# Clustered attention and MLP on one core: a fourth staging buffer, two copies on GpSimd, and the exponential's bias on ScalarE

## The chip, the cores and the metric

The kernel runs on one core of a Trainium2 chip. The core has a matrix engine (TensorE; PE in the profile, with its weight loads under PEld), three engines for elementwise work (VectorE or DVE, ScalarE or ACT, GpSimd or POOL), a queue for DMAs (SyncE or SP) and 16 DMA engines. Each engine takes its instructions in order and waits on semaphores for the others. The metric is device time in microseconds of one execution. The time before is 1006.37 us, the median of 3 runs from 1002.96 to 1007.54.

## The reference

Attention in which a query sees only keys of its own cluster, followed by an MLP with a squared relu:

```python
B, H, S, D = 4, 8, 768, 64            # 16 clusters a head
q_assign = argmax(einsum('bhsd,hcd->bhsc', q_n, c_n))      # rows normalized
k_assign = argmax(einsum('bhsd,hcd->bhsc', k_n, c_n))
scores = (q @ k.T) / sqrt(D); scores = where(q_assign == k_assign, scores, -1e9)
attn = exp(scores - max(scores)); attn = attn / (sum(attn) + 1e-9)
x = (attn @ v) rearranged to (B*S, H*D) = (3072, 512)
h = x @ w_in                           # (512, 2048)
out = (s * relu(h)**2 + b) @ w_out     # (2048, 512)
```

All inputs and the output are float32. `w_in` and `w_out` arrive as 8-byte elements (the kernel reads them as pairs of 32-bit integers), 16 MB in all.

## The kernel before

**Split numbers.** To keep float32 accuracy at the matrix engine's float16 speed, every operand is held as a high half and a low half in float16, and a product takes three matmuls (high with high, high with low, low with high). For the scores, a key tile `ka` holds high and low halves side by side (128 columns), a second one `kb` holds the high halves again beside a column block with the key's one-hot cluster; the queries have `qa` (low halves, and a copy of the high halves) and `qb` (high halves, and the one-hot). A DMA transpose turns each of the four into `KA`, `KB`, `QA`, `QB`. So `QA` times `KA` plus `QB` times `KB` is the whole masked score.

**Units and steps.** The attention is cut into 192 units of 128 queries by 768 keys. In turn `i` of the main loop (line 699) unit `i` gets its scores (`scores`, L455), its maxima (`maxima`, L464), and its exponential (`exps`, L471 and L474); unit `i-1` gets the high half of its probabilities (`high`, L119) and the low half (`low`, L497) and goes through a DMA transpose to `PT` (L499); two units at a time are multiplied by the values (`values`, L516 to L518) and normalized (L524 to L528). The MLP runs 21 turns behind (`LAG`): step `m = i - 21` takes one of 16 blocks of the hidden layer for 256 tokens: `mlp_in` (L574), relu and two squares on ScalarE (L581 to L584), the low half on GpSimd (L589), and `mlp_out` (L601). The last 21 steps of the MLP have no attention beside them.

**Weights.** `weights()` is a loop over 32 tiles, `w_in` and `w_out` in turn, that is advanced two turns with each turn of the main loop (three at the start). `fetch` takes a 512 KB tile into a staging buffer `wst` (tag "stage", 3 buffers); `rebase` (L203, L205, ScalarE) and `narrow` (L209, L210, VectorE) make float32 out of the 8-byte elements; `bound` collects the magnitudes (L216 or L221, L222) and puts the sign back (L223, GpSimd). Tile `i` is fetched in turn `i`, rebased and narrowed in turn `i+2`, bounded in turn `i+3`. The split of the weights into halves (`wsplit`, L267 and L269) needs the bounds over all tiles, and is called from turn 17 on, one block a turn.

**Keys and queries.** `prep_k` and `prep_q` load, find the scale, split (`split`, L185 on ScalarE and L187 on VectorE), copy the high halves to their second place (L325 for keys, L375 for queries, both VectorE), start the transposes of `ka` and `qa` (L329, L379), compute the cluster assignments (`onehot`, L288 to L294) and start the transposes of `kb` and `qb` (L342, L392). For the first batch they run partly ahead of the main loop; for the others they are spread over the turns of the batch before. `kb` of batch 0's first pair of heads and of all pairs of batches 1 to 3 is one tile that is kept for the whole kernel (`kb_kept`), so that a copy into it must wait until the transpose out of it (L342) has landed. Other large working tiles (`p`, `ph`, `PT`, `qn`, `qa`, `qb`, `ka`) share 11 buffers of tag "big".

**Order.** A planner orders the instructions of each engine from the order of the program, priorities (the first 20 units come first) and its own estimate of times, and sets the semaphores. DMAs are all issued on SP, in order, so one that waits for its buffer holds up those behind it. `last_split` holds the last instructions of the latest split, behind which some early preparation is ordered.

Of the kernel before, what the change touches and what calls it, by code (L numbers as in the profile page):

```python
# [8 lines left out]
F16 = mybir.dt.float16  # L9
BF16 = mybir.dt.bfloat16  # L10
F32 = mybir.dt.float32
I32 = mybir.dt.int32
U32 = mybir.dt.uint32
AF = mybir.ActivationFunctionType
ALU = mybir.AluOpType
# [11 lines left out]
def tile_cluster_attention_mlp(ctx, tc, q, k, v, cent, w_in, w_out, s_in, b_in, out):  # L27
# [28 lines left out]
    def const(shape, dt, name):  # L56
        return cp.tile(shape, dt, tag=name, name=name)
# [120 lines left out]
    def split(hi, lo, src, f, early):  # L178
        if early:
            A.activation(src, src, AF.Copy, scale=f)  # L180
            last_split[1] = A.activation(hi, src, AF.Copy)
            yield
            G.tensor_tensor(lo, src, hi, op=ALU.subtract)
        else:
            last_split[1] = A.activation(hi, src, AF.Copy, scale=f)  # L185
            yield
            V.scalar_tensor_tensor(lo, src, f, hi, op0=ALU.mult, op1=ALU.subtract)  # L187

    def fetch(p):
        ft = p // 2  # L190
        if p % 2 == 0:
            w = wi[ft] = weight_tile(f"wi{ft}")
            src = w_in.bitcast(I32)[:, ft * 2 * P : (ft + 1) * 2 * P].rearrange("(t p) f -> p t f", p=P)
        else:
            w = wo[ft] = weight_tile(f"wo{ft}")
            src = w_out.bitcast(I32)[ft * P : (ft + 1) * P, :].rearrange("p (a f) -> p a f", a=KT)
        st = sb.tile([P, KT, P, 2], I32, tag="stage", name=f"wst_{p}", bufs=3)
        load(st.rearrange("p a f w -> p a (f w)"), src)
        return {"w": w, "st": st, "p": p, "ft": ft}

# [27 lines left out]

    def weights():
        live = {}  # L230
        for i in range(2 * NF + 3):
            if 0 <= i - 3:
                bound(live[i - 3])
                narrowed[0] += 1
            if 0 <= i - 2 < 2 * NF:
                rebase(live[i - 2])
                narrow(live[i - 2])
            if i < 2 * NF:
                live[i] = fetch(i)
            if i < 2 * NF + 2:  # L240
                yield

    def finish_w_in():
# [52 lines left out]
    KS = {}  # L296
    KSM = {}
    QS = {}
    kb_kept = const([P, 2, T, 2, D], F16, "kb")

    def prep_k(b, hp):
        kb = kb_kept
        if b == 0 and hp > 0:
            kb = sb.tile([P, 2 * T, P], F16, tag="big", name=f"kb_{hp}", bufs=BIGN).rearrange("p (h t) (e d) -> p h t e d", h=2, e=2)
        n = f"{b}_{hp}"
        kn = sb.tile([P, 2, T, D], F32, tag="kv", name=f"kn_{n}", bufs=5)
        load(kn, k[b, 2 * hp : 2 * hp + 2].rearrange("h (p t) d -> p h t d", t=T))
        yield
        if hp == 0:
            KSM[b] = sb.tile([P, 4, NP], F32, tag="ksm", name=f"ksm_{n}", bufs=2)  # L310
        sm = [KSM[b][:, e, hp : hp + 1] for e in range(4)]
        km = columns(1, f"k{n}")
        absmax(km, kn.rearrange("p h t d -> p (h t d)"))
        if b:
            yield
        allmax(sm[1], km, f"k{n}", "m" if b or not hp else "h")
        yield
        scale2(sm[2], sm[1])
        inverse2(V, sm[3], sm[2], 22)
        if b == 0 and hp > 0:  # L320
            ka = sb.tile([P, 2 * T, P], F16, tag="big", name=f"ka_{hp}", bufs=BIGN).rearrange("p (h t) (e d) -> p h t e d", h=2, e=2)
        else:
            ka = sb.tile([P, 2, T, 2, D], F16, tag="big", name=f"ka_{n}", bufs=BIGN)
        yield from split(ka[:, :, :, 0, :], ka[:, :, :, 1, :], kn, sm[2], False)
        last_split[0] = V.tensor_copy(kb[:, :, :, 0, :], ka[:, :, :, 0, :])  # L325
        KA = sb.tile([P, 2 * T, P], F16, tag="KA", name=f"KA_{n}", bufs=5)
        KB = sb.tile([P, 2 * T, P], F16, tag="KB", name=f"KB_{n}", bufs=5)
        KS[(b, hp)] = (KA, KB)
        last_turn[0] = nc.sync.dma_start_transpose(KA, ka.rearrange("p h t e d -> p (h t e d)"))  # L329
        yield  # L330
        yield
        pa = (ps_m if b or not hp else ps_h).tile([P, 512], F32, tag="m" if b or not hp else "h", name=f"pk_{n}")
        for h in range(2):
            hc = slice((2 * hp + h) * C, (2 * hp + h + 1) * C)
            for t in range(T):
                i = h * T + t
                o = pa[:, i * C : (i + 1) * C]
                nc.tensor.matmul(o, KA[:, i, :], cT[:, 0, hc], start=True, stop=False)
                nc.tensor.matmul(o, KA[:, i, :], cT[:, 1, hc], start=False, stop=True)
        mk = kb.rearrange("p h t e (r c) -> p (h t) e r c", c=C)[:, :, 1, :, :]  # L340
        yield from onehot(pa, 2 * T, f"k{n}", mk, BIG, -BIG)
        last_turn[0] = nc.sync.dma_start_transpose(KB, kb.rearrange("p h t e d -> p (h t e d)"))  # L342

    def prep_q(b, c, hq):
        n = f"{b}_{c}_{hq}"
        nh = 4
        qn = sb.tile([P, 2 * T * P // 2], F32, tag="big", name=f"qn_{n}", bufs=BIGN)[:, : nh * CT * D].rearrange("p (h t d) -> p h t d", h=nh, t=CT)
        load(
            qn, q[b, nh * hq : nh * hq + nh].rearrange("h (p t) d -> p h t d", t=T)[:, :, c * CT : (c + 1) * CT, :]
        )  # L350
        yield
        prs = slice(2 * hq, 2 * hq + 2)
        sm = sb.tile([P, 4, 2], F32, tag="qsm", name=f"qsm_{n}", bufs=3)
        qm = columns(2, f"q{n}")
        absmax(qm, qn.rearrange("p (j h) t d -> p j (h t d)", j=2))
        if b + c:
            yield
        allmax(sm[:, 1, :], qm, f"q{n}", "m" if b or c else "h")
        yield
        f = sm[:, 2, :]  # L360
        scale2(f, sm[:, 1, :])
        V.tensor_tensor(f, f, KSM[b][:, 3, prs], op=ALU.min)
        V.tensor_tensor(sm[:, 1, :], f, KSM[b][:, 2, prs], op=ALU.mult)
        inverse2(V, sm[:, 3, :], sm[:, 1, :], -3)
        qa = sb.tile([P, 2 * T * P], F16, tag="big", name=f"qa_{n}", bufs=BIGN)[:, : nh * CT * 2 * D].rearrange("p (h t e d) -> p h t e d", h=nh, t=CT, e=2)
        qb = sb.tile([P, 2 * T * P], F16, tag="big", name=f"qb_{n}", bufs=BIGN)[:, : nh * CT * 2 * D].rearrange("p (h t e d) -> p h t e d", h=nh, t=CT, e=2)
        both = []
        for j in range(2):
            hs = slice(2 * j, 2 * j + 2)
            both.append(split(qb[:, hs, :, 0, :], qa[:, hs, :, 0, :], qn[:, hs], sm[:, 2, j : j + 1], b + c == 0))  # L370
        for z in zip(*both):
            yield
        for z in both:
            next(z, None)
        V.tensor_copy(qa[:, :, :, 1, :], qb[:, :, :, 0, :])  # L375
        QA = sb.tile([P, nh * CT, P], F16, tag="QA", name=f"QA_{n}", bufs=2)
        QB = sb.tile([P, nh * CT, P], F16, tag="QB", name=f"QB_{n}", bufs=2)
        QS[(b, c, hq)] = (QA, QB, sm)
        nc.sync.dma_start_transpose(QA, qa.rearrange("p h t e d -> p (h t e d)"))  # L379
        yield  # L380
        yield
        pa = (ps_m if b or c else ps_h).tile([P, 512], F32, tag="m" if b or c else "h", name=f"pq_{n}")
        for h in range(nh):
            hc = slice((nh * hq + h) * C, (nh * hq + h + 1) * C)
            for t in range(CT):
                i = h * CT + t
                o = pa[:, i * C : (i + 1) * C]
                nc.tensor.matmul(o, QA[:, i, :], cT[:, 0, hc], start=True, stop=False)
                nc.tensor.matmul(o, QA[:, i, :], cT[:, 2, hc], start=False, stop=True)
        mk = qb.rearrange("p h t e (r c) -> p (h t) e r c", c=C)[:, :, 1, :, :]  # L390
        yield from onehot(pa, nh * CT, f"q{n}", mk, BIG, 0.0)
        nc.sync.dma_start_transpose(QB, qb.rearrange("p h t e d -> p (h t e d)"))  # L392
# [41 lines left out]
                    yield  # L434


    LIFT = 14.0 * math.log(2.0)
    units = [(b, c, hp, t, h) for b in range(B) for c in range(NCH) for hp in range(NP) for t in range(CT) for h in range(2)]
    NU = len(units)
    U = {}  # L440
# [25 lines left out]
    def exps(i):  # L466
# [1 line left out]
        sm = SM[i // 4]  # L468
        bi = sm[:, 1, j : j + 1]
        u = U[i]  # L470
        V.tensor_scalar(bi, sm[:, 0, j : j + 1], u["scale"], LIFT, op0=ALU.mult, op1=ALU.add)  # L471
        p = sb.tile([P, S], F32, tag="big", name=f"p_{i}", bufs=BIGN)
        total = {"accum_out": sm[:, 2, j : j + 1]} if i < RAW else {}
        last_exp[0] = A.activation(p.rearrange("p (a b) -> p a b", a=2), u["sc"], AF.Exp, bias=bi, scale=u["scale"], **total)  # L474
# [117 lines left out]
    def mlp_out(b, c, ft):  # L592
# [9 lines left out]
                                 start=(ft == 0 and gl + wl == 0), stop=(ft == NF - 1 and gl == 1))  # L602
        if ft == NF - 1:
            _, e, acc = MS.pop((b, c))
            o = sb.tile([P, CT, DM], F32, tag="stage", name=f"o_{n}", bufs=3)
            if b + c == 0:
                column_sums()
            for t in range(CT):
# [151 lines left out]
```

## Time and profile before

| | us | |
|---|---|---|
| median of 3 runs | 1006.37 | 1002.96 to 1007.54 |
| the profiled execution | 1002.93 | its span is 1001.3 |
| mean granted TensorE clock | 0.932 | of full speed |

The profile is of one execution. Its page gives busy times of the engines, the span in 40 slices, the chain of work that ended last, and groups of instructions. A group's row names the line, the engine, the operation, the tiles out and in with their shapes and the count, then the total busy us and the mean ns of one, then the idle time of its engine just before them with what ended it:

```profile
L464 DVE TENSOR_REDUCE ssm<-sc 128x1 f32<-128x768 f32 x192 | 181.3, 949 | 24.9 <-PE sc L455 24.8
L474 ACT ACTIVATE p<-sc,ssm,qsm 128x768 f32<-128x768 f32 x192 | 188.4, 981 | 63.0 <-DVE ssm L471 37.2
L589 POOL TENSOR_TENSOR g<-r,g 128x256 f16<-128x256 f32 x192 | 137.2, 715 | 128.2 <-ACT r L584 117.7
```

So the 192 maxima take 181.3 us of VectorE, 0.949 us each. Idle time of an engine that isn't the bottleneck costs nothing. A row of a timeline or of the chain of waits gives start, length and what ran; a row of waits gives who waited for whom, total us, how many times, and the longest. Matmuls are pipelined, so that a busy PE need not be at its peak.

### The profile page before, as it was taken

Reading aid. Unit: us, or ns where it says so; the run is one execution under the profiler, and the core shown is the slowest. Engines: PE = TensorE matmul, PEld = TensorE weight load, DVE = VectorE, ACT = ScalarE, POOL = GpSimd, SP = SyncE. Lnnn points to the kernel's source line nnn. Section 1 sums busy time; section 2 is a strip of 40 time slices with the busy share of each in tenths; the row PEclk is TensorE's granted clock in tenths of the full one; section 3 lists DMA queues with packets and bytes.
Section 4 is the critical chain, followed back from the end, with each engine's and each line's share of the span. In section 5 each row is a group of like instructions: output and inputs, shape, how many; then the busy total and the mean of one; then the engine's idle time right before and its main releaser. Section 6 shows DMA issues by size and latency. Waiting matters only on the chain.

```text
span 1001.3 us, 22497 instructions
## 1 busy us (share of the span) xinstructions
PE 845.3 (84%) x8625; PEld 584.2 (58%) x8625; DVE 692.5 (69%) x1707; ACT 675.5 (67%) x1224; POOL 524.9 (52%) x502
## 2 busy tenths in 40 slices
PE   1568436977989899998899999997888998999997
PEld 1346224644566666665566776665666666767764
DVE  6797978889687756768877657687877665574100
ACT  3577666766477777766577877765777775778553
POOL 1225754555255666555466656643566664666422
PEclk9966656999999999999899999998999999999999
DMA  7875986686686976799898679987878776979300
GB/s 186 199 199 171 236 203 117 117 188 116 130 152 134 174 133 117 143 204 173 171 154 155 144 126 170 180 163 159 156 146 169 128 125 129 151 120 160 47 22 22
DMA packets 450299, 147.36 MB, mean 147 GB/s; under 512 B 417936, under 2 KB 446608, under 8 KB 450192
## 3 DMA queue, kind: packets, MB, share of 16 engines
q1 hardware_dynamic: 450192, 145.93, 74.8%
q8 instruction: 67, 1.10, 0.4%
q14 instruction: 40, 0.33, 0.1%
HBM read 35.69 MB, written 6.29 MB: 42 GB/s over the span
## 4 chain that ended last, share of the span: by engine, by line
PE 43%; DVE 19%; DMA 17%; ACT 8%; issue 5%; POOL 3%; SPq 1%; POOLq 0%; DVEq 0%; ACTq 0%
PE h L574 15%; PE acc L601 14%; PE sc L455 6%; DVE ssm L464 4%; DMA PT<-ph 3%; DMA QB<-qb 3%; DMA qn<-in_q_dram 2%; ACT p L474 2%; PE px L516 2%; PE px L518 2%; PE px L517 2%; DMA wst<-in_moe_w_out_dram 2%; DMA KB<-kb 2%; DMA kn<-in_k_dram 2%; POOL ph L497 2%
## 5 line engine op out<-in xcount | busy, mean ns | idle before, releaser
L497 POOL TENSOR_TENSOR ph<-p,ph 128x768 f16<-128x768 f32 x184 | 310.3, 1687 | 225.3 <-ACT ph L119 173.1
L574 PE MATMUL h<-x,wis 128*128 128x256 f16 x2304 | 295.7, 277 | 7.2 <-ACT r L581 2.9
L601 PE MATMUL acc<-wos,g 128*128 128x512 f16 x1152 | 297.4, 380 | 4.0 <-POOL g L589 3.6
L574 PEld LDWEIGHTS <-wis 128*128 128x128 f16 x2304 | 225.2, 99 | 66.0 <-issue 7.7
L474 ACT ACTIVATE p<-sc,ssm,qsm 128x768 f32<-128x768 f32 x192 | 188.4, 981 | 63.0 <-DVE ssm L471 37.2
L589 POOL TENSOR_TENSOR g<-r,g 128x256 f16<-128x256 f32 x192 | 137.2, 715 | 128.2 <-ACT r L584 117.7
L464 DVE TENSOR_REDUCE ssm<-sc 128x1 f32<-128x768 f32 x192 | 181.3, 949 | 24.9 <-PE sc L455 24.8
L581 ACT ACTIVATE r<-h,cf 128x256 f32<-128x256 f32 x192 | 90.0, 469 | 126.0 <-PE h L574 94.5
L601 PEld LDWEIGHTS <-g 128*128 128x128 f16 x1152 | 104.2, 98 | 86.1 <-POOL g L589 7.6
L119 ACT ACTIVATE ph<-p 128x768 f16<-128x768 f32 x174 | 144.8, 832 | 13.0 <-DMA PT<-ph 9.0
L516 PE MATMUL px<-vh,PT 128*128 128x65 f16 x1104 | 122.0, 198 | 22.7 <-DVE qsm L98 7.4
L455 PE MATMUL sc<-KA,QA 128*128 128x384 f16 x384 | 104.2, 351 | 32.9 <-ACT p L474 29.6
L517 PE MATMUL px<-vl,PT 128*128 128x64 f16 x1104 | 122.1, 195 | 0.0
L518 PE MATMUL px<-vh,PT 128*128 128x65 f16 x1104 | 121.6, 196 | 0.0
L517 PEld LDWEIGHTS <-PT 128*128 128x128 f16 x1104 | 105.3, 101 | 24.7 <-issue 16.4
L516 PEld LDWEIGHTS <-PT 128*128 128x128 f16 x1104 | 105.4, 100 | 23.3 <-issue 14.5
L455 PE MATMUL sc<-KB,QB 128*128 128x384 f16 x384 | 102.5, 352 | 17.9 <-DMA QB<-qb 16.1
L518 PEld LDWEIGHTS <-PT 128*128 128x128 f16 x1104 | 105.3, 100 | 3.1
L583 ACT ACTIVATE g<-r 128x256 f16<-128x256 f32 x192 | 79.4, 413 | 3.9
L584 ACT ACTIVATE r<-r 128x256 f32<-128x256 f32 x192 | 79.0, 412 | 3.6
L455 PEld LDWEIGHTS <-QA 128*128 128x128 f16 x384 | 37.2, 103 | 62.4 <-issue 37.4
L455 PEld LDWEIGHTS <-QB 128*128 128x128 f16 x384 | 38.4, 104 | 50.0 <-DMA QB<-qb 22.3
(152 smaller groups left out, 1031.8 us busy)
## 6 DMA issues: line engine op xcount, KB each, us to landing
wst<-in_moe_w_in_dram SPq DMA_DIRECT2D x16, 512.0 KB, 4.5
wst<-in_moe_w_out_dram SPq DMA_DIRECT2D x16, 512.0 KB, 4.0
kn<-in_k_dram SPq DMA_DIRECT2D x16, 384.0 KB, 3.8
qn<-in_q_dram SPq DMA_DIRECT2D x24, 256.0 KB, 3.8
vn<-in_v_dram SPq DMA_DIRECT2D x16, 384.0 KB, 4.1
out_dram<-o SPq DMA_DIRECT2D x12, 512.0 KB, 4.1
PT<-ph SPq DMA_TRANSPOSE x184, 4.0
x<-xn SPq DMA_TRANSPOSE x48, 2.8
```

The costliest lines, as they stand in the source:

```text
L119: A.activation(dst, src, AF.Copy)
L455: last_score[0] = nc.tensor.matmul(sc[:, e, :HALF], X[:, col, :], y[:, h * S + e * HALF : h * S + (e + 1) * HALF], start=st, stop=not st)
L464: last_max[0] = V.tensor_reduce(SM[i // 4][:, 0, j : j + 1], U[i]["sc"], axis=AX.XY, op=ALU.max, negate=True)
L474: last_exp[0] = A.activation(p.rearrange("p (a b) -> p a b", a=2), u["sc"], AF.Exp, bias=bi, scale=u["scale"], **total)
L497: G.tensor_tensor(u["ph"][:, 1, :], u["p"], u["ph"][:, 0, :], op=ALU.subtract)
L516: nc.tensor.matmul(o1, PT[:, kt, :], vh[:, h, kt, : D + 1], start=(kt == 0), stop=False)
L517: nc.tensor.matmul(o, PT[:, kt, :], vl[:, h, kt, :], start=False, stop=False)
L518: nc.tensor.matmul(o1, PT[:, T + kt, :], vh[:, h, kt, : D + 1], start=False, stop=(kt == T - 1))
L574: nc.tensor.matmul(ph[:, :CW], WSP[ft][0][:, wl, kt, :], XS[(b, c, kt)][:, :, xl, :], start=(i == 0), stop=(i == len(terms) - 1))
L581: A.activation(r, ph[:, :CW], AF.Relu, scale=MS[(b, c)][0])
L589: G.tensor_tensor(g[:, 1, :], r, g[:, 0, :], op=ALU.subtract)
L601: nc.tensor.matmul(acc[:, t, :], g[:, gl, rows], WSP[ft][1][:, wl, :], start=(ft == 0 and gl + wl == 0), stop=(ft == NF - 1 and gl == 1))
```

## The change

Three things change together.

1. The staging buffers go from 3 to 4 (for the output tiles too, which share the tag), and the weights' loop is one turn longer: tile `i` is still fetched in turn `i`, but rebased and narrowed in turn `i+3` and bounded in turn `i+4`.
2. The copies of the high halves (24 for queries, 16 for keys) are issued on GpSimd instead of VectorE. The kept `kb` goes; each `kb` is now a tile of the shared tag "big". `last_split[0]` now names the split's own subtraction, since the copy is no longer VectorE's.
3. The exponential's bias (the negated maximum times the scale plus a constant) is an activation on ScalarE with the scale and the constant read from memory, instead of a multiply-add on VectorE with the constant in the instruction.

```diff
@@ split
-            V.scalar_tensor_tensor(lo, src, f, hi, op0=ALU.mult, op1=ALU.subtract)
+            last_split[0] = V.scalar_tensor_tensor(lo, src, f, hi, op0=ALU.mult, op1=ALU.subtract)
@@ fetch
-        st = sb.tile([P, KT, P, 2], I32, tag="stage", name=f"wst_{p}", bufs=3)
+        st = sb.tile([P, KT, P, 2], I32, tag="stage", name=f"wst_{p}", bufs=4)
@@ weights
-        for i in range(2 * NF + 3):
-            if 0 <= i - 3:
-                bound(live[i - 3])
+        for i in range(2 * NF + 4):
+            if 0 <= i - 4:
+                bound(live[i - 4])
                 narrowed[0] += 1
-            if 0 <= i - 2 < 2 * NF:
-                rebase(live[i - 2])
-                narrow(live[i - 2])
+            if 0 <= i - 3 < 2 * NF:
+                rebase(live[i - 3])
+                narrow(live[i - 3])
             if i < 2 * NF:
                 live[i] = fetch(i)
-            if i < 2 * NF + 2:
+            if i < 2 * NF + 3:
                 yield
@@ prep_k
-    kb_kept = const([P, 2, T, 2, D], F16, "kb")
-        kb = kb_kept
-        if b == 0 and hp > 0:
-            kb = sb.tile([P, 2 * T, P], F16, tag="big", name=f"kb_{hp}", bufs=BIGN)...
...
+        kb = sb.tile([P, 2 * T, P], F16, tag="big", name=f"kb_{n}", bufs=BIGN)...
         yield from split(ka[:, :, :, 0, :], ka[:, :, :, 1, :], kn, sm[2], False)
-        last_split[0] = V.tensor_copy(kb[:, :, :, 0, :], ka[:, :, :, 0, :])
+        G.tensor_copy(kb[:, :, :, 0, :], ka[:, :, :, 0, :])
@@ prep_q
-        V.tensor_copy(qa[:, :, :, 1, :], qb[:, :, :, 0, :])
+        G.tensor_copy(qa[:, :, :, 1, :], qb[:, :, :, 0, :])
@@ exps
-    LIFT = 14.0 * math.log(2.0)
+    lift = const([P, 1], F32, "lift")
+    G.memset(lift, 14.0 * math.log(2.0))
-        V.tensor_scalar(bi, sm[:, 0, j : j + 1], u["scale"], LIFT, op0=ALU.mult, op1=ALU.add)
+        A.activation(bi, sm[:, 0, j : j + 1], AF.Identity, scale=u["scale"], bias=lift)
@@ mlp_out
-            o = sb.tile([P, CT, DM], F32, tag="stage", name=f"o_{n}", bufs=3)
+            o = sb.tile([P, CT, DM], F32, tag="stage", name=f"o_{n}", bufs=4)
```

More of the change, by code (lines that the diff above doesn't have):

```diff
@@ L298, in tile_cluster_attention_mlp @@
     QS = {}
-    kb_kept = const([P, 2, T, 2, D], F16, "kb")
     def prep_k(b, hp):
-        kb = kb_kept
-        if b == 0 and hp > 0:
-            kb = sb.tile([P, 2 * T, P], F16, tag="big", name=f"kb_{hp}", bufs=BIGN).rearrange("p (h t) (e d) -> p h t e d", h=2, e=2)
         n = f"{b}_{hp}"
@@ L319, in prep_k @@
         inverse2(V, sm[3], sm[2], 22)
[L320 to L323, printed above, removed]
+        ka = sb.tile([P, 2 * T, P], F16, tag="big", name=f"ka_{n}", bufs=BIGN).rearrange("p (h t) (e d) -> p h t e d", h=2, e=2)
+        kb = sb.tile([P, 2 * T, P], F16, tag="big", name=f"kb_{n}", bufs=BIGN).rearrange("p (h t) (e d) -> p h t e d", h=2, e=2)
         yield from split(ka[:, :, :, 0, :], ka[:, :, :, 1, :], kn, sm[2], False)
-        last_split[0] = V.tensor_copy(kb[:, :, :, 0, :], ka[:, :, :, 0, :])
+        G.tensor_copy(kb[:, :, :, 0, :], ka[:, :, :, 0, :])
         KA = sb.tile([P, 2 * T, P], F16, tag="KA", name=f"KA_{n}", bufs=5)
```

## The prediction

> **What bounds the kernel now.** I read the page's busy times first, then the busy times of each engine by stage, then the chain of waits of the first stages.
>
> ```profile
> PE 845.3 (84%) x8625; PEld 584.2 (58%) x8625; DVE 692.5 (69%) x1707; ACT 675.5 (67%) x1224; POOL 524.9 (52%) x502
> ...
> 25.00:175.00 150.00, 83.59 (x662) 59.95 (x661) 130.04 (x291) 100.45 (x180) 72.69 (x54) 0.67 0.77 188
> 175.00:250.00 75.00, 63.45 (x594) 39.95 (x592) 67.10 (x139) 53.46 (x98) 41.15 (x34) 0.95 0.71 139
> 250.00:425.00 175.00, 161.97 (x1751) 112.69 (x1751) 123.35 (x310) 119.60 (x217) 96.11 (x90) 0.98 0.77 141
> 425.00:525.00 100.00, 88.12 (x971) 60.12 (x969) 77.59 (x191) 67.81 (x119) 53.00 (x49) 0.97 0.93 175
> 525.00:650.00 125.00, 121.09 (x1303) 84.89 (x1299) 84.61 (x215) 95.35 (x171) 78.52 (x73) 1.00 0.84 155
> 650.00:750.00 100.00, 86.00 (x943) 59.78 (x942) 77.17 (x196) 66.48 (x119) 49.86 (x47) 0.95 0.84 158
> 750.00:925.00 175.00, 166.22 (x1814) 116.82 (x1813) 108.64 (x277) 128.23 (x232) 108.05 (x96) 0.99 0.79 139
> ```
>
> In a row of stages the columns are the stretch, its length, then the busy time (instructions) of PE, PE's weight loads, DVE, ACT and POOL, the granted clock, the DMA share and GB/s. The reader is to see three kinds of stage. From 525 to 650 and from 750 to 925 PE is busy 97% and 95% of the time: there PE sets the pace, and work taken from another engine gains nothing. From 25 to 175, where the weights arrive and are narrowed, PE is at 56%, at a clock of 0.67, and DVE is the fullest engine at 87%; so it is from 175 to 250 (89%), where the weights are split. At the change of batch (425 to 525, 650 to 750) PE falls to 88% and 86%, and DVE carries 77 us of 100.
>
> ```profile
> by line: DMA wst<-in_moe_w_out_dram 11.6%; issue 7.6%; DMA wst<-in_moe_w_in_dram 5.5%; ACT p L474 4.4%; DVE ssm L464 4.4%; ACT wsg L205 3.5%; DVE wo L210 3.5%; DVE wi L209 3.2%; DVE qa L187 2.6%; ACT wi L203 2.4%; ACT wo L216 2.3%; DVE wi L
> ...
> 82.66 0.56 ACT wsg L205
> 83.24 4.11 DMA wst<-in_moe_w_out_dram
> 87.38 0.67 ACT wo L203
> 88.05 0.56 ACT wsg L205
> 88.64 3.38 DMA wst<-in_moe_w_out_dram
> 92.04 0.66 ACT wo L203
> ```
>
> The first line is the chain of waits of the stretch 25 to 175, the others are six of its pieces (start, length, what). Arriving weights are the largest item: 11.6% + 5.5% of 150 us = 25.7 us. The pieces show why: a rebase on ACT (L203, L205) ends, a staging slot comes free, the next fetch goes out, 3.4 to 4.1 us later it lands, and ACT at once rebases what has landed. With three slots the fetch isn't early enough.
>
> ```profile
> ACT wo L203 <- DMA wst<-in_moe_w_out_dram: 7.9, 7, 2.6
> ACT wi L203 <- DMA wst<-in_moe_w_in_dram: 6.2, 6, 1.6
> ...
> 26.90 0.65 ACT L203 ACTIVATE wi<-wst 128x512 f32<-128x512 f32 x1
> 142.77 0.67 ACT L203 ACTIVATE wo<-wst 128x512 f32<-128x512 f32 x1 [0.18 <-DMA wst<-in_moe_w_out_dram]
> ...
> L574 PE MATMUL h<-x,wis x2304: 269/273/421, 148.5 to 992.6; 128*128 128x256 f16 x192
> ```
>
> By the table of waits (total us, times, longest) ACT itself idled 14.1 us for these landings. The next two rows, from ACT's timeline, are the first and the last of the 32 rebases: 116 us for 31 steps, 3.7 us a tile. The last row says that the MLP's first matmul starts at 148.5 us, 5 us behind the last rebase: the weights set when the MLP begins.
>
> **The change part by part.** The sum is made against the profiled execution, 1002.93 us (span 1001.3).
>
> *Fourth place.* A fetch still goes out when the tile four places back, formerly three, has been narrowed, which is one turn of the weights' loop earlier in both kernels; but its data is wanted three turns later and not two. So no fetch is added, SP queues the same DMAs in the same order, and only the time for landing grows by a turn. At 3.7 us a tile a turn is about as long as a landing, so one more turn covers it. Ceiling: the 25.7 us of the chain. Floor: nothing, if DVE is late instead. DVE has only 150 - 130 = 20 us idle in that stage, and it can't use all. I take the middle below ACT's own 14.1 us of idle: **-10 us**. The last tile is narrowed one turn later; at most 3.7 us of it stands on the path to the first split, I take **+2**.
>
> *The bias moves from DVE to ACT.*
>
> ```profile
> L471 DVE TENSOR_SCALAR ssm<-ssm,qsm 128x1 f32<-128x1 f32 x192 | 38.2, 206 | 1.6
> L143 ACT ACTIVATE cs<-cs 128x1 f32<-128x1 f32 x1 | 0.2, 203 | 1.0 <-DVE cs L142 1.0
> L185 ACT ACTIVATE qb<-qn,qsm 128x256 f16<-128x256 f32 x44 | 20.2, 499 | 13.8 <-DVE qsm L362 13.5
> L181 ACT ACTIVATE qb<-qn 128x256 f16<-128x256 f32 x4 | 1.4, 401 | 0.0
> ...
> 25.00:175.00 150.00, 4.74 (x24) 0.67 0.77 188
> 175.00:250.00 75.00, 2.82 (x14) 0.95 0.71 139
> 525.00:650.00 125.00, 6.34 (x32) 1.00 0.84 155
> 750.00:925.00 175.00, 8.70 (x44) 0.99 0.79 139
> ```
>
> The last four rows are L471 alone by stage. DVE loses 38.2 us. ACT has no row of a one-column operation with a scale and a bias from memory. Below it lies L143, 203 ns, with neither; a scale from memory costs 499 - 401 = 98 ns at one shape. So 203 + 2 x 98 = 0.40 us, which I take; the far end is the 499 of L185. ACT gains 192 x 0.40 = 77 us and goes from 675 to 752 us (75%). In the PE-bound stages that is 32 x 0.40 = 13 us on 95.35 of 125 (87%) and 44 x 0.40 = 18 us on 128.23 of 175 (84%): nearly full, on an engine that works in order. Behind the bias stands the exponential, and behind that the high half, relu and squares. The way from maximum to exponential grows by 0.40 - 0.21 = 0.19 us a unit. PE's other work hides it in those stages; without that cover it costs 76 x 0.40 = 30 us there. I take **+4**.
>
> What DVE gains counts where it is fullest: 4.7 us from 25 to 175, at 87% **-4**; 2.8 us from 175 to 250, with a key's and a query's copy on top (about 0.9 us each, below), while ACT takes on 14 x 0.40 = 5.6 us at 71%: **-3**.
>
> *The copies move to GpSimd.*
>
> ```profile
> L375 DVE COPY qa<-qb 128x512 f16<-128x512 f16 x24 | 21.4, 893 | 0.0
> L325 DVE COPY kb<-ka 128x768 f16<-128x768 f16 x16 | 15.6, 978 | 7.7 <-DMA KB<-kb 7.5
> L375 DVE COPY qa<-qb x24: 277/754/1739, 16.5 to 882.6; 128x512 f16<-128x512 f16 x24
> L108 POOL MEMSET ones<- 128x128 bf16 x1 | 0.2, 205 | 0.0
> L154 POOL MEMSET cnat<- 128x256 f16 x1 | 0.3, 315 | 0.0
> L113 POOL CAST identb<-ident 128x128 bf16<-128x128 f32 x1 | 0.3, 305 | 0.0
> L497 POOL TENSOR_TENSOR ph<-p,ph 128x768 f16<-128x768 f32 x184 | 310.3, 1687 | 225.3 <-ACT ph L119 173.1
> ...
> 425.00:525.00 100.00, 5.53 (x4) 0.97 0.93 175
> 650.00:750.00 100.00, 4.04 (x4) 0.95 0.84 158
> ```
>
> The last two rows are L325 alone. DVE loses 21.4 + 15.6 = 37 us of copying and 7.5 us in which it stood before the one kept `kb` until the transpose out of it had landed. Per copy on POOL: the memsets give (315 - 205)/128 = 0.86 ns a column; from the one CAST, 305 + 384 x 0.86 = 0.64 us for a query and 305 + 640 x 0.86 = 0.86 us for a key. Ends: memset alone, 0.53 and 0.75; the two-operand L497, 1.69. So 24 x 0.64 + 16 x 0.86 = 29 us (25 to 68) on an engine at 52%. The keys' copy has its column of one-hots still to come, so it hides. At a change of batch DVE loses 5.5 or 4.0 us of keys' copies, some 4 us of biases, and its waits: about 10 of its 77 us. PE misses 12 and 14 us there; I give back a quarter, 3 us at each of the two, and 3 more where batch 0 ends (250 to 425): **-9**.
>
> Of the copy's three times in the third row (least, median, most) the same form spans six-fold: DVE is held up. The Trainium skill (GPSIMD Engine Reference, Key points) says that GpSimd shares its SBUF interfaces with VectorE, so that VectorE's two-port modes contend with it; the spread agrees. By that rule the move is partly undone: every copy on GpSimd holds back DVE's other fast forms, at most 29 us times their share of DVE's time, and a DVE copy undisturbed is 0.28 us.
>
> *Buffers.* `kb` of batches 1 to 3 and of the first pair leaves its own place for one of the 11 shared ones (p, ph, PT, query tiles), for some five steps each. Nothing shows it; free to a few us at each batch, **+2**. Output tiles get a fourth buffer: nothing, since they are stored long after.
>
> Sum: -10 + 2 + 4 - 4 - 3 - 9 + 2 = -18 us: 985 us for an execution like the profiled one. That one was 3.4 us under the median of 1006.37, so I predict **988 us**.
>
> **The rivals.**
>
> ```profile
> PE sc L455 <- ACT p L474: 29.6, 20, 4.7
> PE sc L455 <- DMA QB<-qb: 16.1, 12, 3.8
> ```
>
> 1. *ACT becomes the bound* (slower). For it: 87% in a PE-bound stage, and PE waited 29.6 us for exponentials even now. Against it: these waits lie mostly before 250 us, where ACT has a third of its time free. The Trainium skill (ScalarE: Activation LUTs, Rules for kernel authors) advises VectorE rather than ScalarE for adds and multiplies; 0.21 against 0.40 us agrees. If ACT's 0.40 us surfaces on all 76 PE-bound units (+30, not +4), the 0.19 us on the 38 units before 250 (+7) takes back the 7 gained from DVE there, and nothing comes at the batches, then fetch and buffers leave 1002.9 - 8 + 2 + 30 = 1027, or 1012 if half of the 30 shows; with the median's 3.4 that is 1030 and 1015. It decides against the change from 6 / 76 = 0.08 us a unit on, where what fetch and buffers bring is used up.
> 2. *The queries' copies come late* (no change). The copy stands ahead of QA's transpose, the assignments, and QB, for which PE already waits 16.1 us in 12 cases. On POOL it queues behind a 1.69 us L497: 12 x 1.69 = 20 us back, so 985 + 20 = 1005, with the 3.4 us 1008. Against it: the DVE copy itself took 0.89 us, 0.25 more than I give POOL.
> 3. *The fetch was hidden anyway* (a small gain): DVE, not the landing, paces the weights. Then -10 and +2 go: 993, with the 3.4 us 996. For it: DVE at 87%. Against it: ACT sat idle for landings 13 times.
>
> **How the numbers follow.** Forecast 0.50 (988), rival 1 0.20 (1015 to 1030), rival 2 0.16 (1008), rival 3 0.14 (996). About 0.5%, 5 us, is what a measurement of this kernel can tell from no change; that bound lies at 1001 and 1011. Faster 0.50 + 0.12 of rival 3 = 0.62; same 0.16 + 0.02 = 0.18; slower 0.20. At the low end stand the ceiling of the fetch term (15.7 us below mine) and half instead of a quarter of what PE misses at the batches (6.5 us more): 966. At the high end the nearer value of rival 1 is taken in: 1015.
>
> **What would show it.** Right: ACT's waits on `wst` fall from 14.1 us to a few; the first matmul of L574 comes some 10 us before its 148.5 us; the DVE wait for KB is gone; DVE falls to about 617 us, ACT rises to about 750, POOL to about 554; PE stays over 94% in the two PE-bound stages. Wrong: PE at 90% there with waits for p or r, or longer PE waits for QB; a bias that takes over 0.5 us; `wst` waits gone but the same time to the first L574, with DVE over 95% ahead of it.

## The result and the profile after

The changed kernel takes 991.77 us (median of 4 runs, 990.88 to 994.74) beside 1004.66 us for the kernel before (the three runs known ahead and one more): ratio 0.9882, 95% interval 0.9848 to 0.9915. The forecast was 988 with a range of 966 to 1015. The profiled execution has a span of 989.2 us, at a mean granted clock of 0.94 (0.932 before).

The page's busy row of the changed kernel, and the stages shown before (stretch, length, then PE, PE's weight loads, DVE, ACT, POOL, clock, DMA share, GB/s):

```profile
PE 837.6 (85%) x8625; PEld 580.6 (59%) x8625; DVE 672.5 (68%) x1475; ACT 724.9 (73%) x1416; POOL 553.9 (56%) x543
...
25.00:175.00 150.00, 80.34 (x643) 57.97 (x643) 128.57 (x262) 102.67 (x196) 74.71 (x57) 0.69 0.74 187
...
250.00:425.00 175.00, 165.35 (x1792) 114.61 (x1789) 116.61 (x256) 136.06 (x266) 107.26 (x102) 1.00 0.70 147
425.00:525.00 100.00, 87.81 (x949) 59.28 (x946) 80.10 (x172) 70.77 (x135) 54.84 (x55) 0.95 0.86 168
525.00:650.00 125.00, 119.99 (x1299) 84.63 (x1298) 76.45 (x172) 99.28 (x198) 77.96 (x74) 1.00 0.77 155
650.00:750.00 100.00, 88.27 (x983) 61.49 (x980) 80.74 (x176) 76.33 (x147) 60.32 (x58) 0.97 0.77 156
750.00:925.00 175.00, 170.24 (x1846) 119.45 (x1845) 95.38 (x221) 142.91 (x281) 111.60 (x104) 1.00 0.67 140
```

The reader is to see that the early stage, for which the largest term was forecast, is no fuller than before (PE 80 us of 150, against 84), while PE is busier from 250 to 425 (165 against 162, where 3 us had been forecast) and from 750 to 925 (170 against 166, where no gain was forecast). The groups of the moved work, with busy us, mean ns and the idle time before:

```profile
L466 ACT ACTIVATE ssm<-ssm,lift,qsm 128x1 f32<-128x1 f32 x192 | 73.3, 382 | 107.3 <-DVE ssm L459 106.4
L369 POOL COPY qa<-qb 128x512 f16<-128x512 f16 x24 | 17.5, 729 | 0.7 <-DMA PT<-ph 0.7
L319 POOL COPY kb<-ka 128x768 f16<-128x768 f16 x16 | 15.6, 981 | 8.4 <-ACT ka L185 7.5 <-ACT r L576 0.8
```

The single prices were about right: 0.38 us for the bias (0.40 taken), 0.73 and 0.98 us for the copies (0.64 and 0.86 taken). Now the early stage, in the table of waits, ACT's timeline (last rebase) and the instructions of the MLP's first line:

```profile
ACT wi L203 <- DMA wst<-in_moe_w_in_dram: 8.1, 6, 4.3
...
ACT wo L203 <- DMA wst<-in_moe_w_out_dram: 5.7, 6, 2.3
...
148.66 0.65 ACT L203 ACTIVATE wo<-wst 128x512 f32<-128x512 f32 x1
...
L569 PE MATMUL h<-x,wis x2304: 269/273/421, 156.9 to 980.6; 128*128 128x256 f16 x192
```

ACT still idles 13.8 us for landing weights (14.1 before). The last rebase comes at 148.7 us, not at 142.8; the MLP's first matmul at 156.9, not at 148.5. Following relu (L581, now L576) through ACT's timeline shows where the gain arose:

| relu of MLP step | before, us | after, us | difference |
|---|---|---|---|
| 0 | 171.5 | 174.6 | +3.1 |
| 48 | 404.4 | 396.8 | -7.6 |
| 96 | 614.2 | 608.9 | -5.3 |
| 144 | 831.0 | 822.8 | -8.3 |
| 191 | 993.0 | 981.0 | -12.0 |

So the start lost 3 us, and the steps behind it gained 15: 11 of them by step 48, 4 behind step 144. Between steps 48 and 144, which take in the changes of batch at 425 to 525 and 650 to 750 us, it comes out almost as it went in (-7.6, -8.3).

### The profile page after: what moved, and what is told of

It is laid out like the page before. It is cut to its first block, busy times and chain, and to the rows that moved or that the text cites. A ratio compares the mean times of both kernels' runs of the same rounds, so it can differ in the third digit from the quotient of the medians.

```text
span 989.2 us, 22509 instructions
## 1 busy us (share of the span) xinstructions
PE 837.6 (85%) x8625; PEld 580.6 (59%) x8625; DVE 672.5 (68%) x1475; ACT 724.9 (73%) x1416; POOL 553.9 (56%) x543
## 4 chain that ended last, share of the span: by engine, by line
PE 36%; DVE 29%; DMA 13%; ACT 8%; issue 6%; POOL 5%; SPq 2%; DVEq 0%; POOLq 0%; ACTq 0%
PE h L569 13%; PE acc L596 12%; DVE ssm L459 5%; PE sc L450 5%; POOL ph L492 3%; DMA vn<-in_v_dram 2%; DMA qn<-in_q_dram 2%; ACT p L469 2%; DVE qa L187 2%; DMA PT<-ph 2%; DMA kn<-in_k_dram 2%; ACT ph L119 2%; PE px L511 2%; DMA QA<-qa 2%; DVE vl L187 2%
## 5 line engine op out<-in xcount | busy, mean ns | idle before, releaser
L569 PE MATMUL h<-x,wis 128*128 128x256 f16 x2304 | 291.6, 275 | 8.4 <-ACT r L576 5.7
L466 ACT ACTIVATE ssm<-ssm,lift,qsm 128x1 f32<-128x1 f32 x192 | 73.3, 382 | 107.3 <-DVE ssm L459 106.4
L576 ACT ACTIVATE r<-h,cf 128x256 f32<-128x256 f32 x192 | 89.1, 464 | 69.4 <-PE h L569 53.8
L511 PE MATMUL px<-vh,PT 128*128 128x65 f16 x1104 | 120.9, 196 | 16.1 <-DVE xs L523 5.9
L450 PE MATMUL sc<-KA,QA 128*128 128x384 f16 x384 | 100.1, 342 | 35.6 <-ACT p L469 26.3
L511 PEld LDWEIGHTS <-PT 128*128 128x128 f16 x1104 | 103.5, 98 | 23.4 <-issue 13.5
L512 PEld LDWEIGHTS <-PT 128*128 128x128 f16 x1104 | 103.3, 100 | 20.4 <-issue 10.4
L450 PE MATMUL sc<-KB,QB 128*128 128x384 f16 x384 | 100.4, 344 | 11.0 <-DMA QB<-qb 11.0
L513 PEld LDWEIGHTS <-PT 128*128 128x128 f16 x1104 | 103.4, 98 | 4.0
L519 DVE TENSOR_SCALAR ssm<-px 128x2 f32<-128x2 f32 x92 | 14.2, 154 | 98.6 <-PE px L513 98.3
```

Source lines behind the costliest of these rows:

```text
L450: last_score[0] = nc.tensor.matmul(sc[:, e, :HALF], X[:, col, :], y[:, h * S + e * HALF : h * S + (e + 1) * HALF], start=st, stop=not st)
L511: nc.tensor.matmul(o1, PT[:, kt, :], vh[:, h, kt, : D + 1], start=(kt == 0), stop=False)
L512: nc.tensor.matmul(o, PT[:, kt, :], vl[:, h, kt, :], start=False, stop=False)
L513: nc.tensor.matmul(o1, PT[:, T + kt, :], vh[:, h, kt, : D + 1], start=False, stop=(kt == T - 1))
L569: nc.tensor.matmul(ph[:, :CW], WSP[ft][0][:, wl, kt, :], XS[(b, c, kt)][:, :, xl, :], start=(i == 0), stop=(i == len(terms) - 1))
L576: A.activation(r, ph[:, :CW], AF.Relu, scale=MS[(b, c)][0])
```

## The experiments

Twelve kernels were run. All have `kb` in the shared buffers, as the change has. Seven of them and the changed kernel make eight that differ in the three parts alone. "Ratio" is to the kernel before, run on the same chip, with its 95% interval.

### The parts taken out singly

**no_stage**: the changed kernel with three staging buffers and the old turns.

```diff
-name=f"wst_{p}", bufs=4      # i - 3, i - 4 in weights()
+name=f"wst_{p}", bufs=3      # i - 2, i - 3
```

> Copies and bias moved as in the change, but three staging buffers and the old distance of the weights' loop. Theory A (the prediction's sum: the fourth place is worth 8 us): some 8 us slower than the changed kernel, ratio to before about 0.996. Theory B (the fourth place brings nothing, since in the trace of after the last tile is rebased at 148.7 us and not at 142.8; the gain is made behind 200 us by the work that VectorE loses): as fast as the changed kernel or some us faster, ratio 0.982 to 0.988, with the last rebase back near 143 us.

985.04 us, ratio 0.9794 (0.9761 to 0.9828): faster than the changed kernel, so theory A falls. Its last rebase, in ACT's timeline, is at the same place as the changed kernel's:

```profile
149.71 0.65 ACT L203 ACTIVATE wo<-wst 128x512 f32<-128x512 f32 x1
```

The total is a little below theory B's range, and B is wrong in one detail: it wasn't the fourth place that moved the rebase from 143 to 149 us.

**no_bias**: the changed kernel with the bias on VectorE.

```diff
-        A.activation(bi, sm[:, 0, j : j + 1], AF.Identity, scale=u["scale"], bias=lift)
+        V.tensor_scalar(bi, sm[:, 0, j : j + 1], u["scale"], LIFT, op0=ALU.mult, op1=ALU.add)
```

> Fourth place and copies as in the change, but the bias stays on VectorE. Theory A: the bias's move is worth 3 to 5 us net (4 and 3 gained where VectorE is full, a part at the batches, 4 lost on ScalarE): ratio 0.991 to 0.993. Theory B1 (the bias's move makes most of the gain): ratio 0.996 or above. Theory B2 (the copies make it): ratio near 0.988.

1014.91 us, ratio 1.0101 (1.0072 to 1.0129). Without the bias's move the other two parts lose 10 us; beside them the move is worth 23 us. That is B1 and far beyond it.

**no_copies**: the changed kernel with both copies on VectorE, `kb` still in the shared buffers.

```diff
-        G.tensor_copy(kb[:, :, :, 0, :], ka[:, :, :, 0, :])
+        last_split[0] = V.tensor_copy(kb[:, :, :, 0, :], ka[:, :, :, 0, :])
-        G.tensor_copy(qa[:, :, :, 1, :], qb[:, :, :, 0, :])
+        V.tensor_copy(qa[:, :, :, 1, :], qb[:, :, :, 0, :])
```

> Fourth place and bias as in the change, kb in the shared buffers as in the change, but both copies stay on VectorE. Theory A: the copies are worth about 9 us at the batches: ratio about 0.997. Theory B1 (bias): near 0.988 to 0.990. Theory B2 (copies): 0.997 or above.

1002.57 us, ratio 0.9985 (0.9963 to 1.0006): beside the other parts the copies are worth 11 us. B1 alone and B2 alone both fall: bias and copies are both needed. With the copies, `last_split` goes back to its old meaning here. It orders only the early preparation; what it is worth by itself wasn't tried.

**stage_room**: the kernel before with the fourth place and `kb` in the shared buffers (both taken from the change's diff).

> The fourth place alone, with kb moved to the shared buffers to make room for it; bias and copies stay on VectorE. Theory A: 8 us gained by the fetch, up to 2 lost by the buffer: ratio 0.992 to 0.994. Theory B: no gain, ratio 0.998 to 1.005, and ScalarE's waits for landings go without the first matmul of the MLP coming earlier than 148 us.

1007.21 us, ratio 1.0027 (1.0008 to 1.0045): no gain, theory B.

### Each part alone, and VectorE's load given back

**bias_room**, **copies_only**, **room_only**: the kernel before with `kb` in the shared buffers, and of the rest of the change the bias, the copies, or nothing.

> Of the change only the bias on ScalarE, with kb in the shared buffers; three staging buffers, copies on VectorE. If the parts add up: the fourth place cost 7 us beside the others (985.0 to 991.8) and 2.6 us beside nothing, so this kernel should stand 3 to 7 us under the one with both (1002.6): ratio 0.991 to 0.996. Theory P (the bias's gain needs the copies away from VectorE too): 0.997 to 1.002.

1007.86 us, ratio 1.0056 (1.0032 to 1.0079): above both ranges. They had taken it that the fourth place costs time here too, but it brings 0.7% (0.9985 with it, no_copies). Beside room_only, below, the bias alone gains 0.35%, less than the two intervals can tell from nothing; so it is theory P in kind.

> Of the change only the copies on GpSimd with kb in the shared buffers; bias on VectorE, three staging buffers. The kernel with copies and fourth place was at 1.0101. If the fourth place costs its 3 to 7 us here too: ratio 1.003 to 1.007, so the copies alone lose. The prediction's term of -9 us would give 0.991. Theory P (copies and bias gain only together): 1.003 or above.

1018.01 us, ratio 1.0156 (1.012 to 1.0192): theory P; the copies alone gain nothing. They lose 0.65% beside room_only, where the intervals just overlap, and 0.74% with the fourth place (no_bias beside stage_room), where they don't.

> Only kb moved from its kept place to the shared buffers. The prediction gave +2 us for the buffer and -7.5 us of VectorE's waits for the KB transpose, a part of which shows: ratio 0.997 to 1.003. If the shared buffers run short at the batches, 1.005 or above with more waits on PT's transposes.

1011.9 us, ratio 1.0091 (1.0055 to 1.0127): the shared buffer costs 9 us where 2 had been taken. ScalarE's waits for a landing of `PT`, the sign that had been named, rise only from 9.0 to 12.5 us (high half) and from 7.2 to 8.3 (exponential), so how the 9 us arise stays open. With these the eight kernels are complete (ratios):

| copies on | bias on | three staging buffers | four |
|---|---|---|---|
| VectorE | VectorE | 1.0091 | 1.0027 |
| VectorE | ScalarE | 1.0056 | 0.9985 |
| GpSimd | VectorE | 1.0156 | 1.0101 |
| GpSimd | ScalarE | **0.9794** | 0.9882 (the change) |

The parts don't add. Copies on GpSimd cost 0.7% while the bias is on VectorE, and bring 2.6% or 1.0% once it is on ScalarE. The fourth place brings 0.6 to 0.7% in three rows and costs 0.9% in the last. But its effect on the weights is much the same in each row. The last rebase, three buffers beside four, is at 143.2 and 141.7, 142.7 and 141.3, 152.2 and 150.4, 149.7 and 148.7 us: always 1.0 to 1.8 us earlier; the MLP's first relu comes between 0.1 us later and 2.9 us earlier. The first row's two, from ACT's timelines of room_only and stage_room:

```profile
143.25 0.66 ACT L203 ACTIVATE wo<-wst 128x512 f32<-128x512 f32 x1 [0.87 <-DMA wst<-in_moe_w_out_dram]
```

```profile
141.65 0.67 ACT L203 ACTIVATE wo<-wst 128x512 f32<-128x512 f32 x1
```

**after_and_dve**: the changed kernel, with VectorE's old operation put beside the new one.

```diff
+        spare = sb.tile([P, 1], F32, tag="spare", name=f"spare_{i}", bufs=4)
+        V.tensor_scalar(spare, sm[:, 0, j : j + 1], u["scale"], 14.0 * math.log(2.0), op0=ALU.mult, op1=ALU.add)
         A.activation(bi, sm[:, 0, j : j + 1], AF.Identity, scale=u["scale"], bias=lift)
```

> The changed kernel plus, for each unit, the old one-column multiply-add on VectorE with a result that nothing reads: VectorE gets back the 38 us, the exponential doesn't wait for it. Theory V (VectorE's occupancy is what the bias's move relieves): the time goes back towards that of the kernel with the bias on VectorE, ratio 1.000 to 1.010. Theory W (it is the wait of the exponential for a result behind other work in VectorE's queue): near the changed kernel, 0.986 to 0.992.

991.48 us, ratio 0.9895 (0.9857 to 0.9933). The group of the added operation:

```profile
L467 DVE TENSOR_SCALAR spare<-ssm,qsm 128x1 f32<-128x1 f32 x192 | 38.0, 206 | 1.1
```

VectorE has its 192 operations back, and the ratio is the changed kernel's (0.9882) well within the intervals. Theory V falls: relief from these operations isn't what the bias's move earned. VectorE's whole busy time rises only from 672.5 to 680.9 us, since 20 of the 38 us lie under neighbours and the other operations got shorter.

### The early copies, the idle activation, the slot, and the queries alone

**early_dve**: no_stage, with the copies made ahead of the main loop back on VectorE.

```diff
-        G.tensor_copy(kb[:, :, :, 0, :], ka[:, :, :, 0, :])
+        (G if b else V).tensor_copy(kb[:, :, :, 0, :], ka[:, :, :, 0, :])
-        G.tensor_copy(qa[:, :, :, 1, :], qb[:, :, :, 0, :])
+        (G if b or c else V).tensor_copy(qa[:, :, :, 1, :], qb[:, :, :, 0, :])
```

> Copies and bias moved, three staging buffers, but the copies made ahead of the main loop (batch 0's keys, its first queries) stay on VectorE. In all kernels with these on GpSimd the first exponential comes at 41 to 44 us, in those without at 35 to 38. Theory E (the early copies delay the first scores): first exponential back near 36 us and the gain is kept to the end: ratio 0.973 to 0.976. Theory F (the weights, not the first scores, set when the MLP starts): first exponential earlier, MLP start and total unchanged, 0.978 to 0.982.

990.13 us, ratio 0.9865 (0.9841 to 0.9889). From its ACT timeline, the first exponential and the last rebase; then the same first exponential in no_stage:

```profile
37.67 0.99 ACT L469 ACTIVATE p<-sc,ssm,qsm 128x768 f32<-128x768 f32 x1
...
142.66 0.65 ACT L203 ACTIVATE wo<-wst 128x512 f32<-128x512 f32 x1
```

```profile
41.42 0.99 ACT L469 ACTIVATE p<-sc,ssm,qsm 128x768 f32<-128x768 f32 x1
```

With the early copies on VectorE the first exponential comes 4 us earlier and the last rebase 7. The SP timelines show why the exponential does: the first queries' transpose goes out at 18.40 us in the kernel before and at 30.69 us in the changed one, behind KB's, although its copy on GpSimd had ended at 19.25 + 0.61 us (in early_dve it goes out at 18.70, in no_stage at 29.32). First the kernel before, then SP and POOL of the changed one:

```profile
18.40 1.25 SPq L379 DMA_TRANSPOSE QA<-qa  x1
```

```profile
29.19 1.41 SPq L336 DMA_TRANSPOSE KB<-kb  x1
30.69 1.26 SPq L373 DMA_TRANSPOSE QA<-qa  x1
...
19.25 0.61 POOL L369 COPY qa<-qb 128x512 f16<-128x512 f16 x1
```

The copy itself doesn't make it late; the planner queued the transpose behind one that was ready later. That this also sets the weights back isn't shown. In after_and_dve (first two rows) the transpose is as late and the last rebase early; in qcopy (the other two, a run below) it is the other way round:

```profile
30.45 1.25 SPq L373 DMA_TRANSPOSE QA<-qa  x1
...
143.52 0.66 ACT L203 ACTIVATE wo<-wst 128x512 f32<-128x512 f32 x1
```

```profile
17.62 1.24 SPq L373 DMA_TRANSPOSE QA<-qa  x1
...
148.10 0.67 ACT L203 ACTIVATE wo<-wst 128x512 f32<-128x512 f32 x1
```

So the last rebase moves by 5 us even with an edit that leaves the weights and the copies alone, beside which the 1.0 to 1.8 us of the fourth place are small. Theory E doesn't hold, since the 7 us aren't kept, and neither does F: the MLP's first matmul comes at 148.7 us rather than at no_stage's 155.2, and the total is worse. The last relu of early_dve's profiled execution is at 976.4 us, that of no_stage at 976.2, and by the medians early_dve is slower.

**bias_on_both**: copies_only with ScalarE's activation put beside VectorE's, its result unread; the exponential still takes VectorE's.

```diff
+        spare = sb.tile([P, 1], F32, tag="spare", name=f"spare_{i}", bufs=4)
+        A.activation(spare, sm[:, 0, j : j + 1], AF.Identity, scale=u["scale"], bias=lift)
         V.tensor_scalar(bi, sm[:, 0, j : j + 1], u["scale"], LIFT, op0=ALU.mult, op1=ALU.add)
```

> Copies on GpSimd, three staging buffers, the bias used by the exponential on VectorE as before, and beside it the same activation on ScalarE with a result that nothing reads. Theory W (the exponential's result must not come through VectorE's queue): like the copies alone or slower by ScalarE's load, 1.012 to 1.025. Theory O (only the order and pace that the planner makes of a ScalarE that stops at each maximum counts, not where the bias comes from): near 0.98 to 0.99.

995.65 us, ratio 0.9915 (0.9889 to 0.9942): 192 useless activations make the copies-only kernel 22 us faster. Theory W falls; theory O's range is met within the interval. By the ratios 24 of the 36 us between copies_only and no_stage come back. The other 12 don't, and may belong to VectorE's operations or to the path of the bias. The two changes of batch, first in copies_only, then in bias_on_both:

```profile
425.00:525.00 100.00, 84.44 (x901) 58.16 (x899) 70.80 (x179) 63.09 (x110) 53.57 (x52) 0.93 0.86 162
...
650.00:750.00 100.00, 83.67 (x894) 57.56 (x893) 69.15 (x177) 62.49 (x110) 50.90 (x51) 0.93 0.89 158
```

```profile
425.00:525.00 100.00, 88.00 (x987) 61.31 (x985) 81.44 (x195) 73.78 (x143) 58.91 (x57) 0.98 0.84 177
...
650.00:750.00 100.00, 88.04 (x998) 61.36 (x995) 83.99 (x199) 76.08 (x147) 60.09 (x58) 0.98 0.76 155
```

In the same 100 us PE gets through 987 and 998 matmuls rather than 901 and 894, and the granted clock is 0.98 rather than 0.93. The added activation made the planner lay out another order: with the added operations left out, the longest order that ScalarE's instructions have in common in the two traces holds 983 of 1224 (by tile names without numbers, so at most that many match). A different order is not yet the reason, though: between the changed kernel and after_and_dve, whose times agree, it is 984. The added ones also stop ScalarE at the maximum, 88 times in bias_on_both (the first row below; 74 times in the changed kernel), so its idle time lies more at the maximum and less at relu. Whether the order or these stops bring the gain wasn't separated. The table of waits of bias_on_both, then of copies_only:

```profile
ACT spare L468 <- DVE ssm L460: 111.0, 88, 9.6
...
ACT r L579 <- PE h L572: 57.7, 49, 5.2
```

```profile
ACT r L575 <- PE h L568: 99.7, 77, 7.9
ACT p L468 <- DVE ssm L465: 48.0, 25, 11.5
```

**slot_only**: no_stage with four staging buffers, the turns as with three.

```diff
-name=f"wst_{p}", bufs=3
+name=f"wst_{p}", bufs=4
```

> Copies and bias moved; four staging buffers, but tiles rebased two turns after their fetch as before, so that a fetch needs a buffer freed two turns ago and not one. If SP's wait for a buffer, with all DMAs queued behind it, is what the early stage loses: last rebase 5 to 10 us earlier than with three buffers (149.7 us), ratio 0.970 to 0.976. If VectorE paces the weights (prediction's rival 3): last rebase within 2 us, ratio 0.978 to 0.985.

986.37 us, ratio 0.9844 (0.9819 to 0.9869). The last rebase is at 145.4 us, 4.3 earlier than in no_stage, between the two theories' figures; the total isn't faster than no_stage, whose interval it overlaps.

**qcopy**: bias_room with only the queries' copies on GpSimd.

```diff
-        V.tensor_copy(qa[:, :, :, 1, :], qb[:, :, :, 0, :])
+        G.tensor_copy(qa[:, :, :, 1, :], qb[:, :, :, 0, :])
```

> Bias on ScalarE, only the queries' copies on GpSimd, the keys' on VectorE, kb in the shared buffers, three staging buffers. With no copy moved this was 1.0056, with both 0.9794. Prediction's working (keys at the change of batch carry the gain): 1.000 or above. If the queries' copies carry it (24 copies spread over all stages, each ahead of a transpose that PE waits for): 0.980 to 0.988.

1002.5 us, ratio 0.9988 (0.9967 to 1.0008). From 1.0056 with no copy moved, the queries' give 0.7% and the keys' the other 1.9% down to 0.9794: nearer to the prediction's working (the keys' copies carry more), with a smaller part for the queries. The last step also takes in the new meaning of `last_split`.

The best kernel of all is no_stage, the change without its fourth place: ratio 0.9794, where the change has 0.9882, and the intervals don't touch.

## Why the prediction was right, and where not

Direction and size held: -18 forecast by the sum, -13 by the medians. But that is in good part luck. Put together by the ratios of the eight kernels, the errors are as large as the result and cancel:

| part | forecast, us | measured, us |
|---|---|---|
| shared buffer (room_only) | +2 | +9 |
| bias and copies together (room_only to no_stage) | -12 | -30 |
| fourth place beside them (no_stage to the change) | -8 | +9 |
| sum | -18 | -12 |

- **The fetch (-10, +2): failed.** The step that failed is the one that turned the chain's 25.7 us of landings and ACT's 14.1 us of idle into a gain. In three rows of the table the fourth place does bring 6 to 7 us, but beside the other two parts it loses 9; and at the weights the runs show 1.0 to 1.8 us at the last rebase and at most 2.9 at the first relu. ACT's idle for landings hardly shrank (14.1 to 13.8 us). The chain of waits of the changed kernel, from 25 to 175 us, shows what came in the landings' place:

```profile
by line: issue 12.3%; DVE ssm L459 6.8%; DVE wi L210 6.6%; DVE wo L210 6.5%; DMA wst<-in_moe_w_out_dram 5.8%; DMA QA<-qa 5.4%; DVE wi L209 3.5%; DVE wo L209 3.2%; DMA PT<-ph 3.2%; DVE vl L187 2.9%; DMA wst<-in_moe_w_in_dram 2.7%; ACT p L469
```

  Landings hold 5.8% + 2.7% of it, half of the 17.1% before, but VectorE's maxima rose from 4.4% to 6.8%, its narrowing of `wo` (L210) from 3.5% to 6.5%, and "issue" (time for which the profile shows no wait) from 7.6% to 12.3%. That is the floor that the prediction named, VectorE late instead, and rival 3; VectorE at 128.6 of 150 us remains the fullest engine there. That it paces the weights is read from the chain, not tried singly. Nor is an earlier MLP kept: after_and_dve has the MLP's first matmul at 147.1 us, 10 before the changed kernel's, and the same total. The rest of the fourth place's effect, a gain of 0.6% or a loss of 0.9%, arises in part late: between the relus of steps 48 and 72 the changed kernel takes 114.7 us and no_stage 108.6. Why stays open.
- **The bias's price on ScalarE (+4): not seen.** 0.38 us each, but ACT rises only to 724.9 us and not to 752. Its old 675.5 and the new 73.3 make 748.8; about 24 us of the new ones lie under the ends of their neighbours. PE's share of the two PE-bound stages is 96% and 97%, so rival 1 didn't come, and PE's waits for p (L450) are 26.3 us, 29.6 before.
- **VectorE's relief (-4, -3): failed as a reason.** after_and_dve gives the 192 operations back and loses nothing. DVE fell to 672.5 and not to 617 us, for two reasons. First, 617 takes off the whole 75 us of the moved operations, but in the trace before only 50.6 us of that lie under no other VectorE instruction. Second, VectorE's 1475 other instructions cover 672.5 us, 642.0 before. In the five kernels with both copies on VectorE they cover 639 to 657 us, in the eight with all or most on GpSimd 656 to 673. So a part of the growth goes with the copies, but without them it already varies by 17 us. One form alone shows neither. Its row in the list of instructions (least, median, most in ns) before, after, in room_only (no copy on GpSimd) and in copies_only (both copies there):

```profile
L294 DVE TENSOR_SCALAR qb<-oo_q x24: 272/295/1620, 28.5 to 894.3; 128x512 f16<-128x512 f16 x24
```

```profile
L294 DVE TENSOR_SCALAR qb<-oo_q x24: 278/469/1743, 37.4 to 884.8; 128x512 f16<-128x512 f16 x24
```

```profile
L294 DVE TENSOR_SCALAR qb<-oo_q x24: 276/469/1624, 27.5 to 905.6; 128x512 f16<-128x512 f16 x24
```

```profile
L294 DVE TENSOR_SCALAR qb<-oo_q x24: 266/295/1733, 37.2 to 913.5; 128x512 f16<-128x512 f16 x24
```

  The median grows from 295 to 469 ns with the change, but it is 469 with no copy on GpSimd and 295 with both, so it doesn't follow what GpSimd does. The rule of the Trainium skill that was weighed (GPSIMD Engine Reference, Key points: the two engines share their SBUF interfaces) fits the growth that goes with the copies. How much of it is that sharing wasn't tried.
- **The copies (-9): right in size beside the other two parts** (no_copies to the change, -11 us) and in part in place: at the two changes of batch PE is busy 85.0 and 86.4 us of 100 in no_copies, 87.8 and 88.3 in the change. It is wrong as a term of its own: alone they cost 0.7%.
- **The shared buffer (+2): mis-sized;** alone it costs 9 us (room_only). That is the 9 us which the other parts have to earn first.
- **What took the place of the failed terms** is the joint effect of bias and copies: 0.9794 for both, where the two single effects on room_only (-0.35% and +0.65%) would give 1.012. after_and_dve shows that VectorE's operations aren't it, and bias_on_both that two thirds of it (24 of 36 us) need neither that relief nor the bias's path, only an activation at each maximum on ScalarE. That it is the order laid out by the planner, or the stops that this activation makes, is what is left, not what was shown. Which difference it is, and whether an order with the bias on VectorE could be as good, stays open.

Of what was to show the steps: KB's waits on VectorE are gone and POOL is at 553.9 (554 forecast); rival 2 didn't come, since PE's waits for QB fell from 16.1 to 11.0 us:

```profile
PE sc L450 <- DMA QB<-qb: 11.0, 11, 1.9
```

But the first matmul of the MLP came 8 us later and not 10 earlier. By itself that doesn't refute the fetch term, since no_stage, without the fourth place, has it late too (155.2 us); the pair of no_stage and the change, which loses 9 us by it, and the chain of waits do.

## What to carry to other kernels

Where a planner orders the instructions, price the parts of a change together and then take each out singly: here two parts that each do little or harm gave 3% jointly, and a third cost 0.9% beside them while it helped without them. A shift of a few us in one stage isn't yet the effect of a part: an edit elsewhere can move it as far. A transfer that stands on the chain of waits isn't yet a gain; ask which engine would be late by the same amount. To test whether relief of an engine is what helped, put the same work back with a result that nothing reads. And before operations are taken off an engine's busy time, ask how much of them lies under their neighbours.

## What had not been expected of the hardware

Taking 75 us of operations from VectorE lowered its busy time by 20 us: 25 of them had lain under other instructions, and the others cover 30 us more, a part of which goes with the copies on GpSimd. On ScalarE too 24 of the 73 us of new operations lie under their neighbours. And the granted TensorE clock at the changes of batch differed between programs with the same matmuls, 0.93 in copies_only and 0.98 in bias_on_both: the program that keeps PE less busy there also has it run slower.
